# Leftover rows of four batches as seven half-size products, earlier loads, and norms behind both transposes, in a fused attention and SwiGLU kernel

## The chip, the cores and the metric

The kernel runs on one core of a Trainium2 chip. The metric is device time in microseconds (us). Engines: TensorE (PE for matmuls, PEld for loading their stationary operand), VectorE (DVE), ScalarE (ACT), GpSimd (POOL) and SyncE (SP), each with its own queue of instructions in program order. PSUM is the accumulator memory, in eight banks.

## The reference

Per batch and head, `k` and `v` (576 x 64) are summed down to 32 memory rows with softmax weights of `phi`, `q` attends to those, and the result goes through a SwiGLU block.

```python
a   = exp(phi - max(phi, axis=2));  a = a / (sum(a, axis=2) + 1e-9)
k_m = einsum('bhsm,bhsd->bhmd', a, k);   v_m = einsum('bhsm,bhsd->bhmd', a, v)
scores = softmax(q @ k_m.T / sqrt(64))            # 576 x 32
x = (scores @ v_m), heads side by side            # (8*576) x 512
g = x @ w_gate;  h = g * sigmoid(g) * (x @ w_val) # 4608 x 1536
out = h @ w_out                                   # 4608 x 512
```

There are 8 batches, 8 heads, 576 positions; `w_gate`, `w_val` are 512 x 1536, `w_out` 1536 x 512.

## The kernel before

The kernel is software pipelined over batches by hand. For batch `b` it makes `U` (the memory's v rows times the gate and value weights; `u_item`, `u_three`, `u_values`), then 24 gate slots of four 288-column matmuls, each with a sigmoid-linear unit on ScalarE and a product on VectorE, which give `h` in three chunks of four 128-row blocks. `h @ w_out` of batch `b` is done in the next iteration, as filler among other work.

That product takes 512 of the 576 tokens as a 2 x 2 block matrix and uses seven block products for eight (Winograd's form of Strassen's scheme), with sums of `h` (`Ss`) and of weights (`Ts`) made beforehand. Each of the seven is 6 units of 2 matmuls; `take(n)` runs the next n units of the list `backlog`.

```python
def sums(eng, part=(0, 1, 2, 3)):            # per batch and chunk, 128x512 each
    if 0 in part:
        eng.tensor_tensor(out=t[:, 0], in0=A21, in1=A22, op=ALU.add)
    terms = ((t[:, 0], A11), (A11, A21), (A12, t[:, 1]))
    for n in part:
        if n: subtract(eng, t[:, n], *terms[n - 1])
...
sums(nc.vector if end else nc.gpsimd)        # end: chunk 2
```

The last 64 tokens of each batch are left over. `ends()` copies them, for two batches side by side, into `xs[pair]`, and `out_rest(pair, half)` multiplies them with `w_out` plainly, 12 matmuls of 256 columns for each half of the output columns.

```python
for jf in (2 * n, 2 * n + 1):                # n = 0..5
    nc.tensor.matmul(mine["p"], lhsT=xs[pair][:, jf]..., rhs=WO[jf][:, cols], ...)
```

The loop over batches, cut:

```python
for b in range(2, B):
    ...
    backlog += out_rest(b // 2 - 1, b % 2);  run(take(6))     # b > 2
    loads(b)                                  # b > 2: q, phi, k, v of batch b + 2
    for g in range(NG): scores(b, g)
    ops["p1"]();  u_values(b);  run(take(6))
    z_inv_v(b, 0);  norm(b, 0);  ops["c11"]()
    run(take(6))
    phi_exp(b + 1)
    z_inv_v(b, 1);  norm(b, 1)
    run(take(6));  run_late()
    run(take(12))
    ...                                       # b == 2: u_three, out_rest(0, 0), u_values
    g = gv_slots(b)                           # 24 slots
    beside = 0 if last else min(7, len(backlog))
    outs = [lambda: run(take(1)) for _ in range(len(backlog) - beside)]
    streams = [(g, 0, 24), (outs, 4, 24)]     # (items, first slot, last slot)
    load_qT(b + 1);  phi_sum(b + 1)           # phi_sum: b > 2
    streams += [
        (kv_items(b + 1, lambda: (u_item(b, 2, "aava")(), run(take(2)))), KV, KV + 4),
        ([lambda: (run(take(2)), u_three(b + 1), run(take(3)))], 19, 20)]
    spread(*streams)
```

`z_inv_v` makes the inverse softmax denominators with a reducing transpose, a reciprocal and a transpose on VectorE; `norm` multiplies the exponentials by them. `phi_sum` sums exponentials of `phi` on GpSimd, so that `kv_denominators` needs 2 small matmuls where it takes 9 without. `kv_items` runs the k and v sums (72 matmuls), their norm, and the transposition of the result by DMA. Banks of PSUM come from a list of eight, first in, first out.

Of the kernel before, what the change touches and what calls it, by code (L numbers as in the profile page):

```python
# [14 lines left out]
def kernel(  # L15
# [193 lines left out]
    def phi_sum(b):  # L209
# [4 lines left out]
        mark = att.tile([1, 1], BF16, tag="mark", bufs=1, name="t_mark")  # L214
        nc.gpsimd.tensor_copy(out=mark, in_=atts[b - 1, 1][0:1, 0, 0:1])  # L215
# [81 lines left out]
    def kv_items(b, beside=None):  # L297


        def run_sums():  # L300
            o = 2 * D
            p = [bank([128, CH], FP32, f"p_kv{g}") for g in range(NG)]
            kv_denominators(b, p[0][:, o:o + NG])
            kv_sum(b, p, (0, 1))
            kv_reciprocal(b, p[0][:, o:o + NG])
            kv_norm(b, p)
            done(*p)
            if beside:
                beside()

        return [run_sums, lambda: kv_T(b)]
# [273 lines left out]
    def chunk_done(b, c):  # L585
# [21 lines left out]
        end = c + 1 == NCH  # L607
        if (b, c) in ((0, 2), (1, 1), (1, 2)):
            late.append(lambda *part: sums(nc.gpsimd if b else nc.vector, *part))
        else:  # L610
            sums(nc.vector if end else nc.gpsimd)
        if end and b > 1:
            late.append(ends)
        else:
            ends()
        if (b, c) in beside_sums:
            beside_sums[b, c]()

# [4 lines left out]
    }  # L623

# [10 lines left out]
    def store(t_o, b, t0, count, row=0, cols=slice(0, 512), queues=None):  # L635
# [3 lines left out]
        for n, (r0, m, bb, jj, pp) in enumerate(token_segments(b, t0, count)):  # L639
            eng = queues[n % len(queues)] if queues else nc.sync  # L640
            eng.dma_start(out=out_r[bb, jj, pp:pp + m, cols], in_=t_o[row + r0:row + r0 + m])

    def out_rest(pair, half):

        h = DM // 2
        mine = {}
        cols = slice(h * half, h * half + h)

        def unit(n):
            def run():  # L650
                if n == 0:
                    mine["p"] = bank([128, h], FP32, "p_oo")
                for jf in (2 * n, 2 * n + 1):
                    nc.tensor.matmul(  # L654
                        mine["p"],
                        lhsT=xs[pair][:, jf].rearrange("p a t -> p (a t)"),
                        rhs=WO[jf][:, cols],
                        start=(jf == 0),
                        stop=(jf == NJF - 1),
                    )  # L660
                if n == NJF // 2 - 1:
                    t_o = work.tile([128, h], FP32, tag="to", name="t_o")
                    copy("v" if box.get("end") else "a", t_o, mine["p"])
                    done(mine["p"])
                    end = 2 * pair + 2 == B
                    for k in range(2):
                        store(
                            t_o, 2 * pair + k, S - 64, 64, 64 * k, cols,
                            ((nc.sync, nc.scalar)[k],) if end else None,
                        )  # L670

            return run

        return [unit(n) for n in range(NJF // 2)]

    def products(b, by_hand):
# [3 lines left out]
        lo, hi = slice(0, h), slice(h, DM)  # L680

        def A(e, n):
            return lambda c, m, u: hts[b, c][
# [3 lines left out]
        def Sx(n):  # L687
            return lambda c, m, u: Ss[b, c][:, n, m, 128 * u:128 * u + 128]
# [7 lines left out]
        def product(home, lhs, rhs, after):  # L696
            def unit(k):
                c, m = k // 2, k % 2

                def run():  # L700
                    fresh = k == 0 and home not in mine
                    if fresh:
                        mine[home] = bank([128, 2, h], FP32, f"p_o{home}")
                        mine[home, "new"] = True
                    for u in range(2):
# [21 lines left out]
        def keep(name, home):  # L727
            def run():
                nc.scalar.copy(out=tile_of(name, tag=name, bufs=1), in_=mine[home])
# [8 lines left out]
        def both(name, t0, cols):  # L738
            for u in range(2):
                store(mine[name][:, u, cols], b, t0 + 128 * u, 128, cols=cols)  # L740

        def c11():
            t = tile_of("o1", (128, 2, DM), tag="to")
            add(t[:, :, lo], "a", "p1", True)
            if box.get("end"):
                both("o1", 0, lo)

        def c22():
            t = tile_of("o2", (128, 2, DM), tag="to")
            add(t[:, :, hi], "s", "p5")  # L750
            if box.get("end"):
                both("o2", 256, hi)

        def c12():
            t = mine["o1"]
            add(t[:, :, hi], "c", "q6", True)
            both("o1", 0, hi if box.get("end") else slice(0, DM))

        def c21():
            t = mine["o2"]  # L760
            copy("v" if box.get("end") else "a", t[:, :, lo], mine["s"])
            done(mine["s"])
            both("o2", 256, lo if box.get("end") else slice(0, DM))
# [4 lines left out]
        )  # L768
        now = {n: f for n, f in ops.items() if n not in by_hand}
# [6 lines left out]
        if b + 1 == B:  # L776
# [163 lines left out]
    def loads(b):  # L940

        if b + 2 < B:
            load_q(b + 2)
            load_phi(b + 2, nc.gpsimd)
            load_k(b + 2)
            load_v(b + 2)
# [7 lines left out]
    for b in range(2, B):  # L954
        last = b + 1 == B
        exp_tables()
        if b == 2:
# [15 lines left out]
            mark = att.tile([1, 1], BF16, tag="mark", bufs=1, name="t_mark")  # L973
            nc.gpsimd.tensor_copy(out=mark, in_=Ts[2][0:1, 3, 0, 0:1])
# [5 lines left out]
        else:  # L980
            backlog += out_rest(b // 2 - 1, b % 2)
            run(take(6))
        if b > 2:
            loads(b)
# [9 lines left out]
        norm(b, 0)  # L994
# [4 lines left out]
        z_inv_v(b, 1)  # L999
        norm(b, 1)  # L1000
        run(take(6))
        run_late()
        nc.scalar.preload_act_table_set("silu_and_others")
        run(take(12))
        if b == 2:
            u_three(2)
            run(out_rest(0, 0))
            u_values(2)
            backlog = one[36:]
        g = gv_slots(b)  # L1010
        beside = 0 if last else min(7, len(backlog))
        outs = [lambda: run(take(1)) for _ in range(len(backlog) - beside)]
        streams = [(g, 0, 24), (outs, 4, 24)]
        if last:
            streams += [([u_item(b, 2)], 5, 6)]
        if not last:
            load_qT(b + 1)
            if b > 2:
                phi_sum(b + 1)
            else:  # L1020
                streams += [([lambda: loads(2)], 7, 8)]
# [45 lines left out]
```

The softmax here doesn't subtract the row's maximum and nothing guards it: scores larger than these inputs give would overflow.

## Time and profile before

| | |
|---|---|
| time, median of 3 | 236.99 us (236.09 to 237.15) |
| span of the profiled execution | 234.5 us |
| busy, TensorE matmul | 225.9 us |
| busy, VectorE | 187.4 us |
| busy, ScalarE | 172.5 us |
| busy, GpSimd | 135.2 us |
| gate slots of batch 4 | about 127.3 to 144.0 us |
| last matmul ends | about 230.2 us |

The page has the busy shares, slices of the span, the chain of waits that ended last, and groups of instructions by line and shape with the mean duration of one. The timelines list the instructions of one engine in order of time: start, length, engine, line, operation, output and inputs, and in brackets how long the engine sat idle before it and what ended that. Matmuls of TensorE overlap in their records, so start-to-start distances are used for them.

### The profile page before, as it was taken

To read this page: it belongs to the slowest core of one execution; us is meant where nothing else is said; L and a number is where in the kernel's file an instruction comes from. 1 tells how busy PE (TensorE), PEld (TensorE's weight loads), DVE (VectorE), ACT (ScalarE), POOL (GpSimd) and SP (SyncE) were. 2 spreads that over 40 slices of the span, in tenths; PEclk is the share of its full clock that TensorE was granted. 3 is DMA by queue.
4 is the path that set the end of the run, shared out by engine and by line. 5 is a ranking of instruction groups with operands and counts; after the bars stand their busy time and mean duration, and the time that the engine had idled before them with its cause. 6 is when DMAs were issued, how large, how long until landed. Compare 5 with 4: busy or idle time off the path is not lost.

```text
span 234.5 us, 7300 instructions
## 1 busy us (share of the span) xinstructions
PE 225.9 (96%) x2847; PEld 171.3 (73%) x2847; DVE 187.4 (80%) x417; ACT 172.5 (74%) x368; POOL 135.2 (58%) x171
## 2 busy tenths in 40 slices
PE   7998899999999999999999999999999999999992
PEld 2555466778887777887778777877788777878881
DVE  4157699999979697998799878988799879987621
ACT  2758888988447888977898779968897789677310
POOL 8532426999099159654992399267916493029400
PEclk9999999999999999999999999999999999999999
DMA  6999999999974999899559964999313721122134
GB/s 211 205 205 207 198 208 206 228 238 248 207 169 97 252 216 158 166 247 232 137 80 252 214 110 106 225 226 142 110 25 81 132 89 27 31 62 89 33 92 126
DMA packets 42914, 36.84 MB, mean 157 GB/s; under 512 B 15488, under 2 KB 38528, under 8 KB 42880
## 3 DMA queue, kind: packets, MB, share of 16 engines
q0 software_dynamic: 21440, 22.42, 55.0%
q1 hardware_dynamic: 20176, 12.79, 25.8%
q10 hardware_dynamic: 1264, 1.18, 1.6%
q8 instruction: 22, 0.36, 0.6%
q14 instruction: 12, 0.10, 0.1%
HBM read 42.47 MB, written 9.44 MB: 221 GB/s over the span
## 4 chain that ended last, share of the span: by engine, by line
PE 82%; DMA 8%; POOL 4%; DVE 3%; issue 1%; ACT 0%; DVEq 0%; POOLq 0%
PE p_g L514 20%; PE p_v L514 19%; PE p_os L706 16%; PE p_oc L706 8%; DMA t_kv<-in_v_dram 8%; PE p_u L471 5%; PE p_oo L654 5%; PE p_oa L706 4%; PE p_kv L235 2%; POOL t_es L217 1%; POOL t_q L108 1%; PE p_g L400 1%; POOL t_kv L98 1%; DVE t_lz L443 1%; DVE t_z L434 1%
## 5 line engine op out<-in xcount | busy, mean ns | idle before, releaser
L537 DVE TENSOR_TENSOR t_h<-t_sg,p_v 128x288 bf16<-128x288 bf16 x192 | 83.1, 452 | 15.6 <-PE p_v L514 7.6
L514 PEld LDWEIGHTS <-t_U 128*128 128x128 bf16 x768 | 73.7, 98 | 21.7 <-issue 2.9
L531 ACT ACTIVATE t_sg<-p_g 128x288 bf16<-128x288 f32 x192 | 74.5, 423 | 15.9 <-PE p_g L514 9.1
L514 PE MATMUL p_g<-t_A,t_U 128*128 128x288 bf16 x384 | 77.2, 286 | 0.0
L514 PE MATMUL p_v<-t_A,t_U 128*128 128x288 bf16 x384 | 77.0, 286 | 0.0
L706 PEld LDWEIGHTS <-t_S 128*128 128x128 bf16 x384 | 37.4, 98 | 4.5 <-issue 0.2
L601 POOL TENSOR_TENSOR t_S<-t_h 128x512 bf16<-128x512 bf16 x17 | 19.7, 1156 | 35.2 <-DVE t_h L537 35.2
L491 ACT CAST t_U<-p_u 128x512 bf16<-128x512 f32 x53 | 28.0, 608 | 8.9 <-PE p_u L471 8.9
L706 PEld LDWEIGHTS <-t_h 128*128 128x128 bf16 x288 | 27.3, 98 | 7.8 <-issue 4.0
L706 PE MATMUL p_os<-t_T,t_S 128*128 128x256 bf16 x192 | 23.7, 273 | 0.0
L559 POOL TENSOR_TENSOR t_S<-t_S,t_h 128x512 bf16<-128x512 bf16 x17 | 19.6, 1155 | 1.3
L559 POOL TENSOR_TENSOR t_S<-t_h,t_S 128x512 bf16<-128x512 bf16 x17 | 20.1, 1186 | 0.0
L559 POOL TENSOR_TENSOR t_S<-t_h 128x512 bf16<-128x512 bf16 x17 | 19.6, 1155 | 0.0
L471 PE MATMUL p_u<-W,t_kT 64*32 64x512 bf16 (+1 forms) x416 | 15.9, 363 | 0.1
L706 PE MATMUL p_os<-t_T,t_h 128*128 128x256 bf16 x96 | 15.6, 273 | 0.0
L827 PE MATMUL p_warm<-bones 128*128 128x512 bf16 (+2 forms) x43 | 12.9, 427 | 1.7 <-DVE bones L850 1.7
L451 DVE TENSOR_TENSOR t_A<-t_E,t_lz 128x576 bf16<-128x576 bf16 x16 | 13.4, 840 | 0.9 <-ACT t_lz L427 0.3
L654 PE MATMUL p_oo<-WO,t_x 128*128 128x256 bf16 x96 | 14.0, 273 | 0.0
L495 DVE CAST t_U<-p_u 128x512 bf16<-128x512 f32 x19 | 12.4, 683 | 1.6 <-PE p_u L471 1.6
L215 POOL COPY t_mark<-t_A 1x1 bf16<-1x1 bf16 x4 | 0.7, 182 | 20.3 <-DVE t_A L451 20.3
L706 PE MATMUL p_oc<-t_T,t_S 128*128 128x256 bf16 x96 | 12.0, 273 | 0.0
L706 PE MATMUL p_oa<-WO,t_h 128*128 128x256 bf16 x96 | 11.8, 273 | 0.0
(93 smaller groups left out, 309.9 us busy)
## 6 DMA issues: line engine op xcount, KB each, us to landing
t_kv<-in_k_dram POOLq DMA_DIRECT2D x8, 576.0 KB, 10.1
t_kv<-in_v_dram POOLq DMA_DIRECT2D x8, 576.0 KB, 14.4
out_dram<-t_o SPq DMA_DIRECT2D x21, 192.0 KB, 2.6
t_phi<-in_phi_dram POOLq DMA_DIRECT2D x6, 576.0 KB, 7.9
t_q<-in_q_dram POOLq DMA_DIRECT2D x5, 576.0 KB, 7.4
out_dram<-t_o SPq DMA_DIRECT2D x37, 64.0 KB, 2.0
out_dram<-t_o SPq DMA_DIRECT2D x14, 128.0 KB, 5.8
t_q<-in_q_dram POOLq DMA_DIRECT2D x6, 288.0 KB, 11.3
```

Source lines behind the costliest of these rows:

```text
L451: nc.vector.tensor_tensor(out=a, in0=es.pop((b, g)), in1=lzs.pop((b, g)), op=ALU.mult)
L471: nc.tensor.matmul(p[g][32 * i:32 * i + 32, o:o + n], lhsT=kTs[b][64 * g:64 * g + 64, 2, 32 * i:32 * i + 32], rhs=w_part(w, c, i, g, halve ...
L491: nc.scalar.copy(out=t, in_=p)
L495: nc.vector.tensor_copy(out=t, in_=p)
L514: nc.tensor.matmul(p[:, 0:HALF], lhsT=Us[b, c, g][:, o // 2, which, 128 * (o % 2):128 * (o % 2 + 1)], rhs=atts[b, g][:, r], start=(g == 0) ...
L531: nc.scalar.activation(out=sg, in_=gate[:, 0:HALF], func=AF.Silu)
L537: nc.vector.tensor_tensor(out=dst, in0=sg, in1=val[:, 0:HALF], op=ALU.mult)
L559: eng.tensor_tensor(out=out, in0=x, in1=y, op=ALU.subtract)
L601: eng.tensor_tensor(out=t[:, 0], in0=A21, in1=A22, op=ALU.add)
L654: nc.tensor.matmul(mine["p"], lhsT=xs[pair][:, jf].rearrange("p a t -> p (a t)"), rhs=WO[jf][:, cols], start=(jf == 0), stop=(jf == NJF - 1),)
L706: nc.tensor.matmul(mine[home][:, u], lhsT=lhs(c, m, u), rhs=rhs(c, m), start=fresh and u == 0, stop=(k == 5), skip_group_check=u == 1 or n ...
L827: nc.tensor.matmul(p[:, 0:128 * a], lhsT=bones, rhs=x.to_broadcast([128, a, 128]) if a > 1 else bones, start=True, stop=True,)
```

## The change

It has three parts, and small ones that go with them. (1) The leftovers of four batches (two pairs) become a 2 x 2 block matrix of their own and are multiplied in seven products of 6 single matmuls; the first set runs in the gates of batch 4, the second in the gates of batch 7 and at the end. Its sums (`Qs`) are made on GpSimd; in batch 4 `phi_sum` is left out. (2) The loads of batch `b + 3` are issued when chunk 1 of batch `b` is done; those of batch 4 when chunk 0 of batch 2 is done. The sums of chunk 1 are split in two halves around the loads. (3) The two norms of a batch stand behind both transposes. Beside these: where there is a `phi_sum`, the denominators stand behind the k and v sums and the U step; the stores at the end alternate over two queues in one count; and fillers are spread anew.

```diff
+            behind = b in esums
+            if not behind:
+                kv_denominators(b, p[0][:, o:o + NG])
             kv_sum(b, p, (0, 1))
+            if behind:
+                beside()
+                kv_denominators(b, p[0][:, o:o + NG])
...
-            sums(nc.vector if end else nc.gpsimd)
+        elif end:
+            sums(nc.vector)
+            wait_for(t[0:1, 3, 0, 0:1])
+            for part in ((2,), (3,)) if b + 1 == B else ((3,), (2,)):
+                for f in second:
+                    f(nc.gpsimd, part)
+            second.clear()
         else:
+            if c:
+                sums(nc.gpsimd, (0, 1))
+                second.append(sums)
+            else:
+                sums(nc.gpsimd)
...
+        if b == 2 and c == 0:
+            loads(4)
+        if b > 1 and c == 1:
+            loads(b + 3)
+        if b + 1 == B and end:
+            quad_sums(1, (0, 1, 2))
...
+    def quad_sums(qd, parts=(0, 1, 2, 3)):
+        x, y = xs[2 * qd], xs[2 * qd + 1]
...                                          # 128x256 each, three chunks
+                if n == 0:
+                    nc.gpsimd.tensor_tensor(out=t[:, 0], in0=A21, in1=A22, op=ALU.add)
+                elif n == 1:
+                    subtract(nc.gpsimd, t[:, 1], t[:, 0], A11)
+                elif n == 2:
+                    subtract(nc.gpsimd, A21, A11, A21)
+                else:
+                    subtract(nc.vector if qd else nc.gpsimd, t[:, 2], A12, t[:, 1])
...
-            backlog += out_rest(b // 2 - 1, b % 2)
             run(take(6))
-        if b > 2:
-            loads(b)
...
         z_inv_v(b, 0)
-        norm(b, 0)
         ops["c11"]()
...
         z_inv_v(b, 1)
+        norm(b, 0)
         norm(b, 1)
         run(take(6))
         run_late()
+        if b == 4:
+            wait_for(atts[4, 1][0:1, 0, 0:1])
+            quad_sums(0)
...
             u_three(2)
-            run(out_rest(0, 0))
+            run(one[36:])
             u_values(2)
-            backlog = one[36:]
         g = gv_slots(b)
-        beside = 0 if last else min(7, len(backlog))
+        quad = []
+        if b == 4:
+            quad = products(b, (), 0)[0]
+        if last:
+            rest, rest_ops = products(b, (), 1)
+            backlog += rest[:12]
+        beside = 0 if last or quad else min(4, len(backlog))
-        streams = [(g, 0, 24), (outs, 4, 24)]
+        streams = [(g, 0, 24), (quad[:12], 0, 3), (quad[12:], 12, 18.5)]
+        streams += [(outs, 3, 7 if quad else 24)]
...
-            if b > 2:
+            if b > 2 and b != 4:
                 phi_sum(b + 1)
-                ([lambda: (run(take(2)), u_three(b + 1), run(take(3)))], 19, 20),
+                ([lambda: (u_three(b + 1), run(take(2)))], 19, 20),
...
-    run(out_rest(B // 2 - 1, 0))
     ...
     run(backlog)
-    run(out_rest(B // 2 - 1, 1))
+    quad_sums(1, (3,))
+    run(rest[12:])
```

## The prediction

> **What bounds the kernel now.** I read the page's busy shares first, then the busy table by stage, then the timelines of single engines around one batch (batch 4, whose gates run from about 127.3 to 144.0 us). The busy shares and the rows of slices:
>
> ```profile
> PE 225.9 (96%) x2847; PEld 171.3 (73%) x2847; DVE 187.4 (80%) x417; ACT 172.5 (74%) x368; POOL 135.2 (58%) x171
> ...
> PE   7998899999999999999999999999999999999992
> ```
>
> TensorE is busy in every slice but the first and last. Matmul ends are modelled, so I check with the rate: twelve 256-column matmuls take 1.31 us in the chain of waits, 109 ns each, and a pair of 288-column ones 0.245 us. Laid end to end they fill a batch of 25.3 us; there is no large hole to close. The table by stage gives the others' room (columns: stretch, its length, busy us of PE, PEld, DVE, ACT, POOL, clock, DMA share, GB/s):
>
> ```profile
> 118.90:127.50 8.60, 8.60 (x99) 7.26 (x97) 8.31 (x16) 7.50 (x13) 3.91 (x8) 1.00 0.99 186
> 127.50:144.20 16.70, 16.70 (x236) 12.74 (x235) 13.98 (x33) 13.42 (x34) 12.91 (x16) 1.00 0.83 160
> ...
> 218.40:234.50 16.10, 11.76 (x108) 10.28 (x106) 5.52 (x11) 2.13 (x4) 1.45 (x3) 1.00 0.36 91
> ```
>
> Between two batches' gates (first row) VectorE works 8.31 of 8.60 us, a second bound just under the first. Its timeline shows how close:
>
> ```profile
> 119.65 0.42 DVE L601 TENSOR_TENSOR t_S<-t_h 128x512 bf16<-128x512 bf16 x1
> ...
> 123.23 0.76 DVE L451 TENSOR_TENSOR t_A<-t_E,t_lz 128x576 bf16<-128x576 bf16 x1
> ...
> 126.42 0.76 DVE L451 TENSOR_TENSOR t_A<-t_E,t_lz 128x576 bf16<-128x576 bf16 x1
> ```
>
> From the last gate product (ends 119.61) to the second norm (ends 127.18) are 7.57 us without a gap, and TensorE's first gate matmul, which needs that norm, starts at 127.32. So the gates' start hangs on two chains at once, only 0.14 us apart. What decides when the VectorE chain begins is ScalarE at the end of the gates before:
>
> ```profile
> 140.62 2.05 ACT L491 CAST t_U<-p_u 128x512 bf16<-128x512 f32 x4 [0.58 <-PE p_u L471]
> 142.53 0.76 ACT L531 ACTIVATE t_sg<-p_g 128x288 bf16<-128x288 f32 x2
> 143.13 0.43 ACT L331 COPY t_o<-p_oo 128x256 f32<-128x256 f32 x1
> 143.38 0.79 ACT L531 ACTIVATE t_sg<-p_g 128x288 bf16<-128x288 f32 x2
> ```
>
> Four evacuations of the next batch's U, then four gates and one copy, end at 144.17; the last gate product follows at 144.85. GpSimd has room on average, but at the end its unit costs matter:
>
> ```profile
> L559 POOL TENSOR_TENSOR t_S<-t_h 128x512 bf16<-128x512 bf16 x17 | 19.6, 1155 | 0.0
> ...
> t_kv<-in_v_dram POOLq DMA_DIRECT2D x8, 576.0 KB, 14.4
> ```
>
> **What the skill says.** The Trainium skill, "TensorE: Matmul & The Clock Gate", section "Wait — 56ns, not 53.3ns?", gives start to start as the columns over 2.4 GHz plus about 2.5 ns: 109.2 ns for 256 columns. The trace agrees (1.31 us for 12), so a matmul dropped is worth 0.109 us wherever TensorE binds. "GPSIMD Engine Reference", section "4.1 Engine selection", calls two-input elementwise work about twice as slow there as on VectorE; here the same 128x512 subtraction takes 1155 ns on GpSimd and 442 ns on VectorE, 2.6 times. "PSUM — Partial Sum Buffer", section "Specifications (TRN2)", lists 8 banks per partition, which is the list of eight that the kernel hands out in turn; no wait for a bank is named in TensorE's waits before.
>
> **The change, part by part.**
>
> (1) Leftover products. Before: 8 column halves of 12 matmuls = 96. After: 2 sets of 7 products of 6 = 84. Removed 12 x 0.109 = 1.31 us. Batch 5 loses GpSimd's pre-summed denominators, so 9 small matmuls stand for 2: the 9 took 0.30 us, the 2 about 0.19, so +0.11. Net of TensorE's work: -1.2 us. This is all the change can take from TensorE itself, 0.5%. But the work also moves: batches 2, 3, 5, 6 lose 12 matmuls each, batch 4 gains 30, batch 7 keeps 12 in its gates, and the tail goes from 24 to 30.
>
> (2) Batches 3, 5, 6. Of the 24 filler matmuls in their gates 12 stay. Eight of those lost stand before the evacuation of the next U (call its first matmul T): 8 x 0.109 = 0.87 us. VectorE there needs, by its timeline, 1.2 (two output sums) + 19.5 gate products x 0.46 + 1.85 (norm of k, v and one evacuation) = 12.0 us, TensorE after the change 12.83 - 0.87 = 11.96: equal, so some comes back as waiting, say 0.2. After T nothing is won: T = 140.15 to the next gates at 152.55 is 12.4 us now, and that is the ScalarE-VectorE chain. The output copy of 128x512 (592 ns) now falls behind the U evacuations instead of the 410 ns copy. Batch 2 has that very order in the old trace: T = 89.52, second norm done at 101.95, gates going on at about 102.1, 12.5 us. So +0.1 there. Each of the three: -0.87 + 0.2 + 0.1 = about -0.6; together -1.8.
>
> (3) Batch 2 has no filler at all left. Before T -0.87; a PSUM bank that the k, v norm still holds may cost 0.15; after T the copy leaves ScalarE, so its chain is 0.4 shorter. Sum -1.1.
>
> (4) Batch 4: before T 54 filler matmuls for 16, 38 x 0.109 = +4.14, with the denominators +0.11, and the k, v step without filler may wait 0.2 for a bank. After T the chain without a copy saves 0.4. ScalarE gets four more copies (1.6 us) and VectorE three more sums (1.3), both beside 20 us of TensorE. Sum +4.0.
>
> (5) Batch 7's gates: same count, 0.
>
> (6) The tail. Six more matmuls are +0.65. But six of the seven leftover products need sums that GpSimd makes only after the last gate. VectorE's four sums end at about 220.9 (220.79 before); then a mark 0.18, two 128x512 sums 2.3, the copy of leftovers 0.4, and nine 128x256 sums. A 128x256 one is estimated at 0.66 from GpSimd's rows (182 ns for one element, 1155 for 512): 5.9 us. They end at 229.7. TensorE's own work would be at 228.8 when it wants the last third of those, so up to 0.7 more, of which I count 0.4. The end after it (copy, store, 3.9 us from 230.6 to 234.5) is as before. Sum +1.0.
>
> (7) Loads. Batch 4's loads used to be issued at 74.0 to 77.1, now behind chunk 0 of batch 2, from about 89. v lands 14.4 us after issue by its row, so at about 106; batch 4's k, v products stood at 106.2 and come about 1 us earlier now. That may cost 0 to 1.5 us once; I count 0.4. All later loads only gain room.
>
> (8) Both norms behind both transposes: the same nine VectorE operations in the same 7.57 us, and the gates need both norms. The output sum stands 0.76 us earlier, which no one waits for. 0. The denominators behind k, v sums and U: GpSimd's partial sums ended at 131.24 and TensorE took them at once; the step now has 1.6 us of room. That protects (2), and is worth 0.1 at most.
>
> Sum: -1.8 - 1.1 + 4.0 + 0 + 1.0 + 0.4 - 0.1 = +2.4. I do not take it whole. The waits in (2), (4), (6) and (7), some 2 us of it, are on queues whose order was evidently laid out to hide them (which output buffers are reused, which half of the sums comes first in the last batch, the denominators placed after the U evacuations so that the held banks go to the end of the list). I take away half of those: +1.0, that is 238.0.
>
> **The rivals.** *TensorE alone decides.* Then everything but the matmul count is hidden: 237.0 - 1.2 = 235.8. For it: not 1 us of named waits in the gates before; against it: the 0.14 us between the two chains at the gates' start. *VectorE and ScalarE have become the bound in the light batches.* Then batches 2, 3, 5, 6 return almost nothing, batch 4's 4 us stays: 240 to 241. For it: 8.31 of 8.60 us; against it: inside the gates VectorE still has about 2.7 of 16.7 us idle. *The end or a load takes it:* GpSimd's nine sums or the late v each make one hole of up to 1.5 us, whatever the rest does, on top of either.
>
> **Range and chances.** The lower edge is the first rival with a little more from fewer collisions, 235.4; the upper the second, 240.8. Two per cent is 4.7 us: below 232.3 would take four times the work that is removed, above 241.7 both rivals of loss at once. Faster 0.04, same 0.88, slower 0.08.
>
> **What would show it.** Right: batch periods of about 24.6 us for 3, 5, 6 and 29 for batch 4; a TensorE gap of some tenths at the start of each light batch's gates, ended by the second norm; a wait for a leftover sum from GpSimd in the last 6 us. Wrong: periods of 23.9 in the light batches (then VectorE's chain shrank with the filler, and the first rival holds), periods of 25 (the second), or a gap of over 1 us before batch 4's k, v products.

## The result, and the profile after

| | before | after |
|---|---|---|
| time, median | 236.95 us (236.09 to 237.15) | 246.89 us (246.19 to 247.26) |
| span of the profiled execution | 234.5 us | 244.4 us |
| last matmul ends | 230.2 us | 240.4 us |

The ratio is 1.0423, 95% interval 1.0388 to 1.0458: slower by 4.2%, where 238.0 was predicted and the range ended at 240.8.

Busy shares and slices of the kernel after:

```profile
PE 227.8 (93%) x2842; PEld 170.9 (70%) x2842; DVE 189.5 (78%) x426; ACT 173.5 (71%) x368; POOL 146.0 (60%) x192
...
PE   7987999999999999797399999999999999999983
...
PEclk9999999999999999999679999999999999999999
DMA  6999999999963809999799871999020803122243
```

TensorE's row before was a wall of nines; now it has a dip to 7 in the 17th slice (one slice is 6.1 us, so 98 to 104), and one to 7 and 3 in the 19th and 20th (110 to 122). In the 20th and 21st the granted clock falls to 6 and 7. From the 16th to the 19th slice the DMA engines are full. TensorE's list of waits names what it stood for (columns: us in total, times, longest):

```profile
PE p_u L475 <- DMA t_kT<-t_bkv: 5.2, 1, 5.2
...
PE p_oc L742 <- POOL t_S L563: 1.2, 1, 1.2
...
PE p_os L742 <- ACT t_q L767: 0.9, 1, 0.9
```

To place the difference, take the start of each batch's out product (the first `p_os<-WO,t_h` matmuls in TensorE's timeline) and subtract neighbours. The first row counts from batch 1's out product, the last runs to the end of the span:

| period of batch | before | after | difference | predicted |
|---|---|---|---|---|
| 2 | 38.37 | 37.59 | -0.8 | -1.1 |
| 3 | 25.63 | 33.25 | +7.6 | -0.6, and +0.4 for the loads |
| 4 | 25.24 | 29.26 | +4.0 | +4.0 |
| 5 | 25.30 | 24.03 | -1.3 | -0.6 |
| 6 | 25.30 | 24.02 | -1.3 | -0.6 |
| 7 | 23.59 | 23.59 | 0 | 0 |
| end | 16.30 | 17.77 | +1.5 | +1.0 |

Before rounding the differences add up to +9.8 of the 9.9 us between the spans; the predicted column is the working ahead of its discount. Batch 3 alone decides; the prediction gave the loads, its cause, 0.4.

The table by stage of the kernel after (columns as in the prediction) shows two batches' gates and the two bad stretches of batch 3:

```profile
114.00:120.00 6.00, 0.80 (x14) 0.43 (x19) 0.91 (x3) 0.55 (x2) 3.55 (x5) 0.85 1.11 147
120.00:125.70 5.70, 5.70 (x46) 3.19 (x31) 2.73 (x5) 3.94 (x9) 3.08 (x4) 0.56 0.83 131
...
155.00:163.50 8.50, 8.50 (x98) 7.17 (x96) 8.22 (x18) 8.07 (x14) 3.62 (x6) 1.00 1.17 225
163.50:179.00 15.50, 15.50 (x224) 11.61 (x223) 13.03 (x31) 12.61 (x31) 11.11 (x15) 1.00 0.56 109
```

From 114 to 120 every compute engine but GpSimd is all but idle (0.80, 0.91 and 0.55 of 6 us) while the DMA share is over 1: a transfer is awaited. From 120 to 125.7 TensorE counts as busy throughout, but with 46 matmuls: the clock is at 0.56. "Busy" says little there without the clock column. TensorE's timeline at that point shows both the wait and the slow pairs after it:

```profile
119.84 1.48 PE L475 MATMUL p_u<-W,t_kT 64*32 64x512 bf16 x24 [5.20 <-DMA t_kT<-t_bkv]
...
122.57 0.69 PE L518 MATMUL p_v<-t_A,t_U 128*128 128x288 bf16 x2
123.05 0.69 PE L518 MATMUL p_g<-t_A,t_U 128*128 128x288 bf16 x2
```

From one pair to the next is 0.48 us, where it was 0.245 before. In the light batch 5 (last two rows of the table) TensorE fills both stretches, at full clock, and its gates take 15.5 us where batch 4's took 16.7 before.

What is awaited is the transposition of the next batch's normed k, v (`t_kT`). It goes through SyncE's queue, behind that of q. SyncE in the kernel before, then in the kernel after (start, length of the issue):

```profile
104.65 6.00 SPq L121 DMA_TRANSPOSE t_qT<-t_q  x1
110.76 1.65 SPq L289 DMA_TRANSPOSE t_kT<-t_bkv  x1
```

```profile
105.49 8.63 SPq L121 DMA_TRANSPOSE t_qT<-t_q  x1
114.23 2.71 SPq L288 DMA_TRANSPOSE t_kT<-t_bkv  x1
```

Before, `t_kT` landed at 114.4 and TensorE took it at 114.91, so the old kernel passed this point with half a microsecond to spare. After, q's transposition starts 0.8 us later and holds the queue 2.6 us longer, `t_kT` is issued 3.5 us later, and TensorE resumes at 119.84. And why transfers are slow just then is in GpSimd's timeline of the kernel after:

```profile
89.76 0.82 POOL L115 DMA_DIRECT2D t_q<-in_q_dram  x1
...
95.83 0.81 POOL L115 DMA_DIRECT2D t_q<-in_q_dram  x1
...
99.04 1.14 POOL L563 TENSOR_TENSOR t_S<-t_h,t_S 128x512 bf16<-128x512 bf16 x1
100.15 1.15 POOL L563 TENSOR_TENSOR t_S<-t_h 128x512 bf16<-128x512 bf16 x1
```

The loads of batch 4 (chunk 0 of batch 2) and of batch 5 (chunk 1 of batch 2) are issued 6 us apart, two batches' worth back to back; k and v of batch 5 landed 16 to 19 us after their issue. The issues also stand ahead of the second halves of the chunk 1 sums, which is the 1.2 us wait for `t_S`. This is the only place in the loop with two batches' loads in a row: later ones come one batch at a time.

### The profile page after: what moved, and what is told of

Its sections match the earlier page's. It is cut to its first block, busy times and chain, and to the rows that moved or that the text cites. A ratio compares the mean times of both kernels' runs of the same rounds, so it can differ in the third digit from the quotient of the medians.

```text
span 244.4 us, 7326 instructions
## 1 busy us (share of the span) xinstructions
PE 227.8 (93%) x2842; PEld 170.9 (70%) x2842; DVE 189.5 (78%) x426; ACT 173.5 (71%) x368; POOL 146.0 (60%) x192
## 4 chain that ended last, share of the span: by engine, by line
PE 71%; DMA 14%; DVE 8%; issue 2%; POOL 2%; ACT 1%; ACTq 0%; DVEq 0%; POOLq 0%
PE p_g L518 18%; PE p_v L518 18%; PE p_os L742 16%; PE p_oc L742 7%; DMA W<-in_moe_w_val_dram 7%; DMA t_q<-in_q_dram 5%; PE p_u L475 4%; PE p_oa L742 4%; DMA t_kT<-t_bkv 2%; PE p_kv L234 2%; DVE t_A L455 1%; DVE t_o L772 1%; DVE t_z L438 1%; DVE t_lz L447 1%; DVE t_S L563 1%
## 5 line engine op out<-in xcount | busy, mean ns | idle before, releaser
L541 DVE TENSOR_TENSOR t_h<-t_sg,p_v 128x288 bf16<-128x288 bf16 x192 | 82.1, 452 | 19.5 <-PE p_v L518 9.3
L518 PEld LDWEIGHTS <-t_U 128*128 128x128 bf16 x768 | 74.5, 99 | 24.5 <-issue 4.3
L518 PE MATMUL p_g<-t_A,t_U 128*128 128x288 bf16 x384 | 78.3, 289 | 0.2
L518 PE MATMUL p_v<-t_A,t_U 128*128 128x288 bf16 x384 | 78.0, 288 | 0.3 <-DVE t_bkv L270 0.3
L605 POOL TENSOR_TENSOR t_S<-t_h 128x512 bf16<-128x512 bf16 x17 | 19.7, 1157 | 34.9 <-DVE t_h L541 33.3
L495 ACT CAST t_U<-p_u 128x512 bf16<-128x512 f32 x53 | 27.9, 606 | 11.8 <-PE p_u L475 11.0
L475 PE MATMUL p_u<-W,t_kT 64*32 64x512 bf16 (+1 forms) x416 | 16.7, 378 | 5.4 <-DMA t_kT<-t_bkv 5.2
L563 POOL TENSOR_TENSOR t_S<-t_h 128x512 bf16<-128x512 bf16 x17 | 20.1, 1183 | 0.0
L563 POOL TENSOR_TENSOR t_S<-t_h,t_S 128x512 bf16<-128x512 bf16 x17 | 19.5, 1152 | 0.0
L499 DVE CAST t_U<-p_u 128x512 bf16<-128x512 f32 x19 | 12.5, 684 | 7.4 <-PE p_u L475 7.3
L742 PE MATMUL p_os<-t_T,t_h 128*128 128x256 bf16 x96 | 14.9, 279 | 0.3 <-DVE t_o L772 0.3
L892 PE MATMUL p_warm<-bones 128*128 128x512 bf16 (+2 forms) x43 | 12.5, 416 | 1.7 <-DVE bones L915 1.7
L742 PE MATMUL p_oc<-WO,t_S 128*128 128x256 bf16 x96 | 12.0, 273 | 1.2 <-POOL t_S L563 1.2
L475 PEld LDWEIGHTS <-t_kT 64*32 64x32 bf16 x416 | 5.2, 91 | 10.4 <-DMA t_kT<-t_bkv 5.5
L742 PE MATMUL p_oa<-WO,t_h 128*128 128x256 bf16 x96 | 11.8, 273 | 0.0
## 6 DMA issues: line engine op xcount, KB each, us to landing
t_phi<-in_phi_dram POOLq DMA_DIRECT2D x6, 576.0 KB, 10.3
```

What stands on the lines that cost most here:

```text
L475: nc.tensor.matmul(p[g][32 * i:32 * i + 32, o:o + n], lhsT=kTs[b][64 * g:64 * g + 64, 2, 32 * i:32 * i + 32], rhs=w_part(w, c, i, g, halve ...
L495: nc.scalar.copy(out=t, in_=p)
L499: nc.vector.tensor_copy(out=t, in_=p)
L518: nc.tensor.matmul(p[:, 0:HALF], lhsT=Us[b, c, g][:, o // 2, which, 128 * (o % 2):128 * (o % 2 + 1)], rhs=atts[b, g][:, r], start=(g == 0) ...
L541: nc.vector.tensor_tensor(out=dst, in0=sg, in1=val[:, 0:HALF], op=ALU.mult)
L563: eng.tensor_tensor(out=out, in0=x, in1=y, op=ALU.subtract)
```

## The experiments

Theory A: the loads' place makes the hole, through the transpositions, and the idle time then costs a second time through the clock. Rivals: the new products or the moved norms make it; or the hole is only what any three-batches-ahead scheme costs.

### The hole of batch 3

**e6_before_loads.** The kernel before, with the loads alone moved as in the change.

```diff
-        if b > 2:
-            loads(b)                 # batch b + 2, at the head of the batch
+        if b == 2 and c == 0:
+            loads(2)                 # batch 4, behind chunk 0
+        if b > 1 and c == 1:
+            loads(b + 1)             # batch b + 3, behind chunk 1
...
-            else:                    # b == 2, in slots 7 to 8
-                streams += [([lambda: loads(2)], 7, 8)]
```

In this kernel's code `loads(b)` fetches batch `b + 2`.

> The kernel before with only its loads moved as the change moves them (batch 4's behind chunk 0 of batch 2, then each set three ahead behind chunk 1); leftovers, sums, norms and denominators as before. Theory (overlap of loads with q's transposition delays the transposition of k and v): it has the wait at batch 4's U step by itself, 3 to 5 us, and the half clock behind it: 241 to 245 us. Rival (the hole needs the denominators behind the sums or the shorter gates of the change): 236 to 237.5 us.

245.15 us, ratio 1.0339 (1.0311 to 1.0367). Batch 3's period is 34.43, batches 4 to 6 stay as before (25.36, 25.31, 25.29). TensorE waits 4.0 us for `t_kT` and 2.0 for a norm, and the clock falls to 0.57 over the last 5.7 us of the batch. The moved loads alone make the hole; products and norms are not needed for it.

**e3_kT4_on_pe.** The kernel after, with batch 4's k, v transposed on TensorE, as the first batches' are, so that no transposition by DMA is awaited there.

```diff
-        if b > 3:      # transpose t_bkv by DMA
+        if b > 4:
```

> The changed kernel with the loads left as they are, but the normed k and v of batch 4 transposed on TensorE (three matmuls and one copy on VectorE, as for batches 0 to 3) and not by DMA. Theory: what TensorE waited for is this transposition alone, so the 5.2 us wait and the half clock go, and q's own transposition, which landed at 119.4, comes just in time for the scores at about 119.6: 239 to 240 us; the 1.2 us wait for GpSimd's sum in batch 3 stays. Rival (q's transposition is what is late, and the wait only moves to the scores): 242 to 246 us with a wait of some us at the scores of batch 4.

239.32 us, 1.0122 (1.0087 to 1.0158). Batch 3's period falls from 33.25 to 26.10, although q's transposition is as slow as ever (8.56 us). So of batch 3's loss 7.15 us hang on that one wait and what it drags behind it; the 1.2 us wait for the sums stays.

**e4_warm_wait.** The kernel after, with 24 idle matmuls of 512 columns ahead of the U step of batch 3, where TensorE would stand still.

```diff
-  ([lambda: (u_three(b + 1), run(take(2)))], 19, 20),
+  ([lambda: (warm(96 if b == 3 else 0), u_three(b + 1), run(take(2)))], 19, 20),
```

> The changed kernel with 24 idle matmuls of 512 columns (about 5.2 us, results unused) put ahead of the U step that waits, in batch 3 alone. Theory: they fill the wait of 5.2 us, the transposition lands when they end, and the clock does not drop, so the 2.6 us that the half clock cost come back: 244.3 us (243.8 to 245). Rival (the wait is no wait for data but an effect of the order on TensorE, or the lower clock cost nothing): 246.9 to 252 us.

243.91 us, 1.0312 (1.0283 to 1.0342); the period is 30.99, clock 0.999. The transfer comes no earlier, but 2.3 us of the period (3.0 of the time) go: that was the half clock. So the 7.15 are 4.9 of waiting and 2.3 of slow matmuls after it. The Trainium skill, "TensorE: Matmul & The Clock Gate", section "What's actually happening", says that an idle window of about 3.4 us drops the array to half its clock, and that about as much activity brings it back. The trace of after agrees on the drop: 5.2 us of idle time, then 0.48 us instead of 0.245 from one pair of gate matmuls to the next, from 122.1 to 125.0. The full clock was back at about 125, 5 us after TensorE resumed. A 1.2 us wait in the same batch did nothing to the clock.

**e2_loads_as_before.** The kernel after with all loads as in the kernel before, two ahead at the head of a batch.

> The changed kernel with all loads where the kernel before has them (batch 4's in slot 7 of batch 2, the others at the start of the next batch, two ahead); sums, leftovers, norms and denominators as changed. Theory (pile-up at batch 4 alone): the same time as with batch 4's loads alone moved back, within 1 us, 238 us. Rival (loads three ahead help the later batches, where transpositions now find the DMA engines free): slower than that run by 1 to 3 us. Rival (loads have nothing to do with it): 246 us.

253.66 us, 1.0714 (1.0663 to 1.0764), the worst of all. Now three batches wait for `t_kT`, 11.5 us in all, with periods 30.64, 30.95, 30.39. In the changed kernel GpSimd has more to do at the head of a batch (the split sums), so the first issue comes 3.8 us later in the batch than before (97.33 instead of 94.64, with the out product 1.1 us earlier), right ahead of q's transposition, which takes 8.68, 9.46 and 8.53 us. So the change did need another place for its loads, and its rule does well in the kernel after where only one batch is loaded at a time: q's transpositions in batches 4 and 5 took 3.9 and 3.6 us.

**e1_loads4_early.** The kernel after with batch 4's loads back at 74 us, where the kernel before has them; the rest three ahead.

```diff
-        if b == 2 and c == 0:
-            loads(4)
+            elif b == 2:
+                streams += [([lambda: loads(4)], 7, 8)]
```

> The changed kernel with one edit: the loads of batch 4 are issued in slot 7 to 8 of batch 2's gates again, as before; the loads of batches 5 to 7 stay three ahead. Theory (pile-up): batch 4's loads and batch 5's are in flight one behind the other from 90 to 117 us, the transposition of q for batch 4 shares the DMA engines with them and lands 13.9 us after its issue, the transposition of k and v stands behind it in the same queue, and TensorE waits 5.2 us and then runs about 5 us at half clock. Then this kernel has no such wait, keeps its clock at 1.00, and also loses the 1.2 us wait for GpSimd's sum in batch 3: 238 us (236.5 to 239.5). Rival (three ahead is itself too much traffic, whichever batch): the wait stays or moves to a later batch, 243 us or more. Rival (the late step is the denominators behind the k and v sums): 246 us, no change.

241.76 us, 1.0213 (1.0169 to 1.0256): most of the hole is gone, but 2.0 us of waiting for `t_kT` stay, and the time is 2.3 us above the top of the range that theory A gave. Batch 5's loads alone, ending 6.6 us ahead of q's transposition, still stretch it to 6.53 us. A miss in size: not only two batches in a row do harm, one close by does too.

**e5_combo.** e1 and e3 together.

> The changed kernel with two edits: batch 4's loads in slot 7 of batch 2's gates as before, and batch 4's k and v transposed on TensorE. Theory: both holes of batch 3 go, the wait for the transposition (as with the second edit alone, 239.3 us) and the 1.2 us wait for GpSimd's sum behind the load issues: 238.1 us (237.5 to 238.6), batch 3's period about 24.9 us. What is left above 236.5 is then batch 4 (+4.0 us against -1.3 us in each of batches 2, 3, 5 and 6) and the end (+2.2 us). Rival (the wait for GpSimd only hid the second chain, on VectorE): 239.3 us, unchanged.

239.14 us, 1.0094 (1.0074 to 1.0113), a miss by 1 us. The wait for the sums went, and another came. TensorE's waits of this run:

```profile
PE p_g L404 <- DMA t_qT<-t_q: 1.4, 1, 1.4
```

Batch 4's loads at 74 us run beside the transposition of batch 3's q, which takes 8.96 us there (3.93 in the kernel after). The same mechanism, one batch earlier, at another consumer.

**e9_loads_chunk0.** The kernel after with one rule for all loads: two ahead, behind chunk 0 of the gates.

```diff
-        if b == 2 and c == 0:
-            loads(4)
-        if b > 1 and c == 1:
-            loads(b + 3)
+        if b > 1 and c == 0:
+            loads(b + 2)
```

> The changed kernel with every load two batches ahead, issued behind the sums of chunk 0 (one rule for all batches). Theory: the hole of batch 3 comes from load transfers running beside the two transpositions by DMA (q of the next batch, then k and v); behind chunk 0 the loads fall into the stretch between one batch's k, v transposition and the next batch's q transposition, so no wait for the transposed k, v, no drop of the clock and no split sums waiting behind loads. Batch 3's period is then 24.4 to 24.9 us, batches 5 and 6 stay at 24.0, batch 4 at 29.2: 237 to 238 us. Rival: the overlap only moves on (to the transposition of q, or to the batches after), a wait of over 1 us is named in some batch, and the time is 239 or more.

239.08 us, 1.0103 (1.0078 to 1.0128). Batch 3's period is 24.87, inside what was expected, and no transposition is waited for anywhere; the time is 1 us above, since batch 6 takes 24.56, batch 4 29.51 and the end 18.5. SyncE's timeline of this run, at the same place as above:

```profile
104.26 3.03 SPq L121 DMA_TRANSPOSE t_qT<-t_q  x1
...
108.39 1.89 SPq L288 DMA_TRANSPOSE t_kT<-t_bkv  x1
```

VectorE's timeline shows why batch 6 takes half a microsecond more than batch 5 (24.03). The load issues, now behind chunk 0 (167.20 to 170.28), push GpSimd's first chunk 1 sums from the last gates into VectorE's chunk 2 sums, and the first of these takes 1.08 us, where the kernel after has 0.42:

```profile
171.90 1.08 DVE L605 TENSOR_TENSOR t_S<-t_h 128x512 bf16<-128x512 bf16 x1
173.01 0.50 DVE L563 TENSOR_TENSOR t_S<-t_S,t_h 128x512 bf16<-128x512 bf16 x1
```

The norms come later by that much, and TensorE waits 0.4 us for one. Batch 3 has the same picture (four sums in 2.7 us instead of 1.6, a wait of 0.4, and TensorE 0.8 behind its pace in batch 5 from there on). In e15 below no loads are issued in batch 5, and batch 6 takes 24.03.

The runs together give a rule with numbers. The length of q's transposition issue, against the time from the last load issue to its start (in the period of a batch, q of the next one is transposed):

| runs | last load issue ended before it | length of the issue |
|---|---|---|
| before, batch 2 | 2.0 us | 9.3 us |
| e2, batches 3, 4, 5 | 2.5 to 3.1 us | 8.5 to 9.5 us |
| e1, e2, e5, batch 2 | 5.1 to 5.6 us | 8.0 to 9.0 us |
| before, batches 3, 4, 5; e1, batch 3 | 6.6 to 7.8 us | 5.3 to 6.5 us |
| e5, batch 4 | 9.1 us | 5.2 us |
| after, batch 5; e1, batches 4, 5 | 10.3 to 10.8 us | 3.6 to 4.0 us |
| e9, batches 3 to 6 | 11.8 to 14.1 us | 3.0 to 3.6 us |
| before, batch 6 (no loads left) | none | 3.05 us |
| two batches of loads: after, e6, batch 3; e14, e15, batch 5 | 5.7 to 8.4 us | 8.1 to 11.6 us |

"DMA: Bandwidth & Descriptors", section "Issuing engines are not separate DMA queues", of the Trainium skill says that transfers issued from SyncE, ScalarE or GpSimd run on the same 16 engines and interleave. That is what the table shows from outside: the queues differ, the issues still stretch.

**e15_chunk0_tail2** brought the hole back. It is e10 (below) with batch 7's loads moved to chunk 1 of batch 4, 6 us after batch 6's.

> The seven products with loads behind chunk 0 and the stores at the end dealt out anew (238.2), with batch 7's loads issued in batch 4 as well. Theory: batch 6's period falls from 24.57 to 24.0, so 237.6 to 237.8, still above the kernel before, since batch 4 pays 4.3 to 4.5 and the end 1.2. Rival: the two loads in one batch collide with the transpositions of batch 4, and the time is 238.2 or more.

245.35 us, 1.0352 (1.0322 to 1.0382): the rival, and by far, one batch later than it said. Batch 5's period goes from 24.0 to 31.07. SyncE's timeline:

```profile
158.20 8.11 SPq L121 DMA_TRANSPOSE t_qT<-t_q  x1
166.42 2.72 SPq L288 DMA_TRANSPOSE t_kT<-t_bkv  x1
```

TensorE waits 5.1 us for `t_kT` and its clock falls again. Two batches of loads in a row made this hole in batch 3 (after, e6) and in batch 5 (here and in e14).

### The norms, the sums and VectorE

**e8_combo_norm.** e5 with the first norm back between the transposes.

```diff
         z_inv_v(b, 0)
+        norm(b, 0)
         ...
         z_inv_v(b, 1)
-        norm(b, 0)
         norm(b, 1)
```

> The kernel with both edits, and the first norm put back ahead of the output sum and the second transposition, as in the kernel before. Theory (same VectorE work, same end): equal to the two edits alone within 0.5 us. Rival (the order matters because the first norm shortens or lengthens beside GpSimd): differs by over 0.5 us in one direction.

241.96 us, 1.0214 (1.0193 to 1.0234): a miss. The norms' order was expected to be worth nothing and is worth 0.9 us in each of batches 4 to 6 here (24.97 in place of 24.03 in batch 5). VectorE's timeline ahead of batch 6's gates, first of this run, then of the kernel after:

```profile
177.63 1.58 DVE L455 TENSOR_TENSOR t_A<-t_E,t_lz 128x576 bf16<-128x576 bf16 x1
...
181.64 0.76 DVE L455 TENSOR_TENSOR t_A<-t_E,t_lz 128x576 bf16<-128x576 bf16 x1
```

```profile
186.06 1.39 DVE L455 TENSOR_TENSOR t_A<-t_E,t_lz 128x576 bf16<-128x576 bf16 x2
```

In e8 GpSimd makes the second halves of the chunk 1 sums from 176.00 to 178.25, and the first norm beside them takes 1.58 us in place of 0.76. Moved behind both transposes, both norms together take 1.39, as GpSimd is done by then. Transposes and sums that read PSUM, which now stand beside GpSimd, keep their length (0.77, 0.65). "SBUF — State Buffer", section "Who interferes with whom", of the Trainium skill says of SBUF (the on-chip memory of the tiles) that a VectorE instruction with two SBUF inputs contends with a GpSimd instruction that reads SBUF, and that the order of issue decides which one blocks. The trace agrees, for the norm here, which starts during GpSimd's sum of 177.11 to 178.25, and for the sums in e12.

**e11_before_norms.** The kernel before with both norms behind both transposes, and nothing else changed.

> The kernel before with one thing changed: both norms stand behind both transposes. If the norm order is worth something only because the changed kernel's split sums keep GpSimd busy while the first norm runs, this is within 0.5 us of the kernel before (237.0), and its periods are 25.3. Rival: the norm order is worth 0.5 to 1 us per batch by itself, and the time is 2 us or more below.

236.06 us, 0.9975 (0.9957 to 0.9993): periods 25.17 instead of 25.30, as the theory had it. Without the split sums there is little for the move to save: VectorE's chain from its first chunk 2 sum to the end of the second norm is 0.3 us shorter (7.22 instead of 7.53). The time is 0.25% under the kernel before, just clear of noise, and the lowest of all runs.

**e12_before_rest.** The kernel before with the moved norms, the moved denominators and e9's place of the loads, but without the half-size products and the split of the sums.

> The kernel before with the moved norms, the denominators behind the k and v sums and the U step, and loads two batches ahead behind chunk 0, but with the plain leftover products (8 times 12 matmuls) and unsplit sums: all of the change but the seven half-size products. By the changed kernel's terms these products cost 4.0 in batch 4 and 1.5 at the end, and bring 0.7 in batch 2 and 0.6 to 1.3 in each of three others: net 0 to +2. Theory: this run is 235.5 to 237, at or below the same loads with the seven products. Rival: the seven products do pay, and this is 1 us or more above it.

241.71 us, 1.0218 (1.0194 to 1.0243), a clear miss. The periods of batches 3 to 6 are 26.7 to 27.0, and `p_g` waits 4.3 us in seven places for the norms. VectorE's timeline at the head of batch 4:

```profile
120.96 0.68 DVE L606 TENSOR_TENSOR t_S<-t_h 128x512 bf16<-128x512 bf16 x1
121.67 1.26 DVE L564 TENSOR_TENSOR t_S<-t_S,t_h 128x512 bf16<-128x512 bf16 x1
122.86 1.37 DVE L564 TENSOR_TENSOR t_S<-t_h 128x512 bf16<-128x512 bf16 x1
124.16 0.61 DVE L564 TENSOR_TENSOR t_S<-t_h,t_S 128x512 bf16<-128x512 bf16 x1
```

The four chunk 2 sums span 3.8 us; in the kernel before they span 1.6. The load issues (3.1 us) now stand ahead of GpSimd's four chunk 1 sums and push them to 118.96 to 123.95, right beside VectorE's. The split of the sums avoids that: where loads don't stand in between, the first halves run during the last gates, and the second wait until VectorE's sums are done. With the split added (e13, below) the periods of batches 3 to 5 are 25.2 to 25.4.

### The seven products and the end

**e7_combo_tail.** e5, with the stores at the end on SyncE until the leftovers, so that ScalarE's copies do not queue behind store issues.

> The kernel with both edits, and the stores of batch 7's own products at the end all on SyncE's queue, so that ScalarE's queue is free for the copies that TensorE needs; only the leftovers' stores use both. Theory (the seventh products wait because the copy of the sixth stands behind six store issues in ScalarE's queue): the 0.9 us wait there goes, and the time is 0.5 to 1.0 us less than with the two edits alone, about 237.3 us. Rival (GpSimd's nine sums set the end, as I had predicted): 0 to 0.3 us less. Rival (the stores on one queue come to stand at the very end): slower by up to 1 us.

239.13 us, 1.0095 (1.0079 to 1.0112), no gain over e5's 239.14. The 0.9 us wait went and TensorE's last product came 1.0 us earlier in the end stage, but SyncE's queue was then busy with stores to 232.6 and the last ones left at 232.7 to 234.7.

**e10_chunk0_tail.** e9, with one block's stores held back until ScalarE has made its last copies, and the other early ones of the end all on SyncE.

```diff
-            queues = nc.sync, nc.scalar
+            queues = box.get("q", (nc.sync,))
...
-            both("o2", 256, lo if end else slice(0, DM))
+            if end:
+                later.append(lambda: both("o2", 256, lo))
+            else:
+                both("o2", 256, slice(0, DM))
...
-    run(rest[12:])
+    run(rest[12:24])
+    box["q"] = (nc.scalar,);  run(later)
+    box["q"] = nc.sync, nc.scalar
+    run(rest[24:])
```

> The run before this one, with the end's stores dealt out anew: the stores of batch 7's first column blocks on SyncE alone, one block's stores held back until ScalarE has made its last copies, so that those copies do not stand behind store issues. Theory: the 0.9 us wait of the last products for ScalarE's copy goes and no store comes later: 0.5 to 1.2 us less than the run before. Rival: the stores themselves set the end, as when all of them were put on SyncE: within 0.3 us of the run before.

238.24 us, 1.0074 (1.0051 to 1.0097), 0.8 under e9, as expected. It confirms the reading of these lines of ScalarE's timeline in the kernel after:

```profile
234.17 3.50 ACTq L702 DMA_DIRECT2D out_dram<-t_o  x6
237.76 0.37 ACT L767 COPY t_q<-p_os 128x256 f32<-128x256 f32 x1 [5.10 <-DMA out_dram<-t_o]
```

Six store issues hold ScalarE's queue for 3.5 us, and the copy that the last products need stands behind them.

**e13_plain_split, e14_plain_split2, e16_plain_split3.** To get at the net of the seven products: e12 with the split of the sums, which is the change without these products, with e9's place of the loads. e13 left batch 7's copy of leftovers behind GpSimd's second halves; e14 moved it ahead and put batch 7's loads into batch 4, right behind batch 6's; e16 keeps e13's loads, moves the copy and issues batch 7's phi ahead of its q.

```diff
+        elif c:
+            sums(nc.gpsimd, (0, 1))
+            second.append(sums)      # the other two behind VectorE's sums
```

> The run with all of the change but the seven half-size products (moved norms, loads two batches ahead behind chunk 0, denominators behind) had periods of 26.7, because the load issues push the rest of GpSimd's chunk 1 sums into VectorE's chunk 2 sums, which then take 3.8 us for 1.7. This run adds the change's split of those sums and leaves the plain leftover products. Theory: with the split the collision goes, the periods of batches 3 to 6 are those of TensorE's work with 12 matmuls more than the changed kernel's light batches, 24.03 + 1.31 = 25.3, or the 25.2 of the moved norms alone, and the time is 235.5 to 236.7; then the seven half-size products, with the same loads 239.1, cost 2.4 to 3.6 net. Rival: the loss lies in the split or in the loads at chunk 0 themselves: periods of 25.8 or more, 238.5 or above, and the seven products cost nothing net.

> The run with all of the change but the seven half-size products, freed of two waits that it brought in by itself: the copy of batch 7's leftovers goes ahead of the second half sums on GpSimd (they held it up 3.0 us, and the clock halved after), and batch 7's loads are issued one chunk of batch 4 later than batch 6's, not in batch 5 (ScalarE waited 1.7 us for phi). Theory: what is left is TensorE's work at periods of 25.15 to 25.35, so 235.3 to 236.3, level with the moved norms alone (236.1); the seven products with the same loads (239.1) then cost 2.8 to 3.8 net. Rival: another wait takes over, 237.5 or more, and the cost of the seven products stays under 1.6.

> All of the change but the seven half-size products, once more: loads two batches ahead behind chunk 0 for every batch (two batches' loads within 6 us of each other had brought back a 5.4 us wait for the transposed k, v), batch 7's phi issued ahead of its q, and batch 7's leftovers copied ahead of the second half sums. Theory: no wait is left in the loop, periods 25.15 to 25.35 in batches 3 to 6, 235.4 to 236.6; the seven products with the same loads (239.1, or 238.2 with the stores dealt out anew) then cost 2 to 3.5 net. Rival: phi still comes late or another wait takes over, 237.3 or more, and the net of the seven products stays between 0 and 1.5.

e13: 241.63 us, 1.0209 (1.0167 to 1.0252). Periods 25.15, 25.35, 25.15 in batches 3 to 5, as expected, but batch 6 took 26.67 (ScalarE stood 1.7 us for phi, issued 20 us later than in the kernel before), and at the end TensorE waited 3.0 us for the copy, and soon after its clock was at 0.50 (226.8 to 229.3). e14: 243.82 us, 1.0289 (1.025 to 1.0328): the copy was mended, but batch 5 took 34.84, with 5.4 us of waiting for `t_kT`, 1.5 for a copy on ScalarE, and q's transposition at 11.59 us: two batches' loads in a row once more. e16: 237.05 us, 1.0006 (0.9984 to 1.0028). No wait is left in its loop, the periods are 25.15, 25.16, 25.36, 25.15. Its runs spread from 235.22 to 238.62 and the profiled one is a low one (235.41), so the ratio is the better measure.

With the same place of the loads, the version with the seven products (e9) stands at 1.0103 and the one without at 1.0006, and the intervals do not touch. The products cost 0.97%, 2.3 us net; with e10's better end 0.68%, 1.6 us. The profiled spans give more (237.2 and 236.3 against 233.6), so the size is only roughly known, 1.6 to 3.6 by these measures. By periods, e9 against e16, batch 4 pays 4.4 and the end 2.6, and batches 2, 3, 5 and 6 give back 0.9, 0.3, 1.3 and 0.6. A part of the net is the loads' place and not the products: batch 6 gives back 0.5 more where no loads stand ahead of it (e15). No run has the seven products with loads that spare this and make no hole, so what the products cost by themselves stays open.

## Why the prediction was wrong

The step that failed is (7), *"That may cost 0 to 1.5 us once; I count 0.4."* It asked only whether v would land in time for batch 4's k, v products, and it did: no such wait is named after. It never asked what else used the DMA engines while two batches' loads went through. SyncE's transpositions did, with half a microsecond to spare. In the kernel after the step measured 33.25 - 24.87 = 8.4 us (batch 3 after, and in e9): 1.2 of waiting for sums behind the issues, 4.9 of waiting for `t_kT`, 2.3 of half clock. The profile before had the clue: q's transposition at 79.03, 2 us behind a set of loads, took 9.27 us, that at 104.65 6.00, and the same operation in batch 6, without loads beside it, 3.05. The second half of the step, that later loads only gain room, is right: in batches 4 and 5 of the kernel after q's transposition takes 3.9 and 3.6 us, where it took 5.3 and 5.4 before.

The other steps:

- (1) -1.2: holds. TensorE's instruction count falls by 5, which is 12 matmuls less and 7 small ones more.
- (2) -0.6 each: too little. Batches 5 and 6 got -1.28, the full 12 matmuls (1.31). From the gates' start to T, the first matmul of the next U, batch 5 took 11.85 us instead of 12.83, with none of the 0.2 of waiting that was foreseen. From T to the next gates it took 12.17 where 12.5 was expected. The step took VectorE's chain as given there, and it shrank from 7.53 to 7.05 us; 0.3 of that comes with the norms' order (e11), and with the first norm put back beside the split sums (e8) the period is 24.97. Batch 3 without its hole got -0.8 (24.87), for the reason shown in e9. Periods of about 23.9 were the prediction's own sign for its first rival, TensorE alone, and 24.03 and 24.02 came: in batches 5 and 6 that rival held.
- (3) -1.1 for batch 2: -0.8. One product (at 76.05) waits 0.3 us for VectorE, which the step did not have.
- (4) +4.0 for batch 4: +4.0, with a wait of 0.3 us behind the k, v norm, where 0.2 was foreseen.
- (5) batch 7, 0: holds.
- (6) +1.0 for the end: +1.5, and the wait was another. GpSimd's nine sums took 0.64 us each, as estimated, and ended at 237.69; ScalarE's copy, behind store issues, ended at 238.13, and TensorE waited 0.9 us for it. With the stores dealt out anew (e10) the end is 1.2 us longer than before.
- (8) 0: wrong as a mechanism. *"the same nine VectorE operations in the same 7.57 us"* forgets that the split sums put GpSimd beside them; the order is worth 0.9 us in each of batches 4 to 6 with that split (e8) and about 0.1 without (e11).
- The discount: 2.4 was summed and 1.0 kept, because the order of queues looked laid out to hide the waits. Without the hole (e3, e9) the kernel stands at 239.1 to 239.3, where the undiscounted sum of 239.4 was. That is partly luck: in e9 batches 3, 5 and 6 gave back 1.0 us more than their terms, and batches 2, 4 and the end cost 1.8 more.

Of the rivals, the third (*"The end or a load takes it"*) was the right one, through the load, but with 1.5 us for a hole that cost 8.4: it had no term for the clock, and none for the queue.

As to the change itself: its second part is a loss by one clash in one batch, its third part and the split of the sums are sound and belong together, and its first part did not pay in any run here: light batches give back up to 1.3 us each, but batch 4 pays 4.0 and the end 1.5.

## What to carry to other kernels

When loads move, list every transfer in the stretch they move into, above all those that an engine awaits soon, and compare the same transfer's length with and without loads beside it; spread loads of one batch each, well ahead of a transposition. In this kernel, count a long wait of TensorE half again as dear, for the clock that it loses (an estimate from e4, 2.3 us on top of 4.9; waits of 3.0, 4.0 and 5.1 to 5.4 us dropped the clock here, of 1.2 and 2.0 did not). And parts of a change that share an engine's queue (here load issues, sums and norms on GpSimd and VectorE) are not to be priced one by one: loads behind chunk 0 without the split cost 5 us (e12), the norm order 0.9 or about 0.1 us a batch.

## What was not expected of the hardware

- An issue of a transposition on SyncE took 3.0 us alone and up to 11.6 us (e14) behind two batches of loads issued from another engine, and held the next one in its queue back.
- 5.2 us of idle time on TensorE cost another 2.3 us of the period behind it, through the clock at half (e4).
- VectorE's 128x512 sums, 0.42 us each, took up to 1.37 beside GpSimd's sums (e12), and a norm 1.58 in place of 0.76 (e8), while its transposes (0.77) and its sums from PSUM (0.65) did not change.
